# Weight conversion in place, two feed-forward pieces held over, and four first-pair copies on VectorE, in a top-k attention and hardswish kernel

## The chip, the cores and the metric

One Trainium2 chip, one of its cores. The metric is the device time of one launch in microseconds. Three runs of the kernel before took 1567.45, 1564.12 and 1565.65 us; their median, 1565.65 us, is the time before.

## What is computed

Attention over 8 batches and 8 heads (576 rows of width 64) in which each row of scores keeps only its 32 largest entries, followed by a feed-forward block with a hardswish gate over the 4608 rows that result:

```python
scores = scale * np.matmul(q, k.transpose(0, 1, 3, 2))
kth = np.partition(scores, -top_k, axis=-1)[..., -top_k:-top_k + 1]
scores = np.where(scores >= kth, scores, -1000000000.0)
scores = scores - np.max(scores, axis=-1, keepdims=True)
attn = np.exp(scores)
attn = attn / (np.sum(attn, axis=-1, keepdims=True) + 1e-09)
x = np.matmul(attn, v)             # then (B,H,S,D) -> (B*S, H*D)
h = x @ w_in                       # 512 -> 2048
g = h * np.clip(h + 3.0, 0.0, 6.0) / 6.0
out = g @ w_out                    # 2048 -> 512
```

`top_k` is 32. q, k and v are float32. The weights are float64, so each of them reaches the kernel as a pair of 32-bit words, `lo` and `hi`, and is turned into float32 on the chip.

## The kernel before

**Pairs and duos.** Two heads make a pair (`Pair`), two pairs a duo (`Duo`): one tile of 128 query rows (or the 64 rows that are left over, a "rest" duo) of four heads. There are 80 duos, ten in each batch; `m` numbers them. Even batches end with their two rest duos, odd batches begin with them.

**Slots.** The order of the work is written out by hand. The loop of L608 gives each duo eight slots, numbered 8m+i. In a slot VectorE does one round of `top` (L276): eight maxima of a row (`max`, L283) and their removal (`match_replace`, L287), for both heads of a pair; four rounds per pair find the 32 largest. The other steps of a duo hang at fixed slots after its start (the tables of L570 to L583; `usual`, `behind` for the middle of the run, `early` for the first two duos, `soon` for the last two): `shift` (GpSimd), `exp` (ScalarE, L306 to L316), `inverse` (VectorE, L320), `weights` (GpSimd, L330 and the copy of L339 that splits words into halves), `flip` (a transposing DMA on SP's queue, L345), `join` (ScalarE for the duo's first pair, GpSimd for its second, L351), `values` (TensorE, L371), `place` (ScalarE, L381, from PSUM to `xT`). `scores` of the next duo (TensorE, L256 and L262, then ScalarE's copy from PSUM, L271) are issued in slot 1 of a duo, and transposes of a later pair (L182, then copies on ScalarE, L205 to L187) in slot 5 where there is one.

**Pieces.** When both duos of a row tile are placed, `queue` (L471) adds a feed-forward block: 16 pieces. Pieces 0 to 7 compute `h` (L398, two pieces per 512 columns, then ScalarE's L406 and L408 and, two pieces later, GpSimd's gate L412 and L413); pieces 8 to 15 accumulate `acc` (L418), and the last also scales the result (ScalarE, L428) and sends it out (a DMA on SP's queue, L430). `left` counts the pieces not yet issued. At the end of each slot L639 adds 1 to `due` while `left` is over 0 (half as much in slots of a rest duo, a little more when `left` is 24 or over), and `piece` issues that many. A block is queued about every 16 slots, so `left` runs from 16 to 0 and a new block follows at once: in slot order, the block's last piece is issued just before `place` of the next block's second duo.

**Weights.** 32 chunks of 128x512 (16 of `w_in`, 16 of `w_out`) are converted one per slot in the first 33 slots (`convert`, L96; `convert_step`, L522). A chunk is loaded into a tile `st` of the pool `kq` (14 buffers, shared with all the tiles of the attention). Three slots later ScalarE writes |hi| into a tile `a` of the pool `g` (L109), GpSimd clamps it (L110), and ScalarE makes `y` from `lo` (L112); two slots after that VectorE shifts `a` (L118) and merges the sign into the destination (L119), and in the next slot GpSimd adds both (L124). `y` is a PSUM tile (pool `ps_w`, 3 buffers, shared with `h`, `acc` and `pv`) where `early` holds, else the destination itself. L518 makes `early` true for chunks 0 to 15.

**Start.** The first pair is transposed through three `ps_w` tiles (L189 to L202) and ScalarE copies the keys (L195), the first query tile (L196) and the left-over keys (L187). Scores of that pair alone follow (`us == (0,)`, L267), copied out in three parts by ScalarE.

Each engine runs its instructions in program order, and so does SP's queue of DMAs.

Of the kernel before, what the change touches and what calls it, by code (L numbers as in the profile page):

```python
# [8 lines left out]
AF = mybir.ActivationFunctionType  # L9
ALU = mybir.AluOpType  # L10
F32 = mybir.dt.float32
U32 = mybir.dt.uint32
I32 = mybir.dt.int32
# [11 lines left out]
HI_LEAST = 2.0**-15  # L25
HI_MOST = 122880.0 - 2.0**-7
# [3 lines left out]
def kernel(  # L30
# [9 lines left out]
    nc = tc.nc  # L40
    P = nc.NUM_PARTITIONS
# [3 lines left out]
    JP = J * P  # L45
    R = S - JP
    NHP = H // 2
    NFC = FF // P
# [4 lines left out]
    def pool(name, bufs, **kw):  # L53
        return ctx.enter_context(tc.tile_pool(name=name, bufs=bufs, **kw))
# [8 lines left out]
    gpool = pool("g", 8)  # L63
# [24 lines left out]
    def big():  # L88

        return ps_big.tile([P, 5 * 512], F32, tag="big", name="big")  # L90
# [3 lines left out]
    WC = 512  # L94

    def convert(dst, src, early):  # L96

        st = kqpool.tile([P, 2 * WC], U32, tag="kq", name="st")
        nc.sync.dma_start(st[:], src)
        yield
        words = st[:].rearrange("p (n two) -> p n two", two=2)
        lo, hi = words[:, :, 0], words[:, :, 1]
        a = gpool.tile([P, WC], F32, tag="g", name="a")
        y = ps_w.tile([P, WC], F32, tag="w", name="y")[:] if early else dst
        nc.scalar.activation(a[:], hi.bitcast(F32), AF.Abs)  # L109
        nc.gpsimd.tensor_scalar(a[:], a[:], HI_MOST, HI_LEAST, ALU.min, ALU.max)  # L110

        nc.scalar.activation(y, lo, AF.Copy, bias=2.0, scale=2.0**-51)  # L112
        yield

        au = a[:].bitcast(U32)
        nc.vector.tensor_scalar(au, au, 3, None, ALU.logical_shift_left)  # L118
        nc.vector.scalar_tensor_tensor(  # L119
            out=dst.bitcast(U32), in0=hi, scalar=0x80000000, in1=y.bitcast(U32),  # L120
            op0=ALU.bitwise_and, op1=ALU.bitwise_or,
        )
        yield
        nc.gpsimd.tensor_tensor(  # L124
            dst.bitcast(I32), a[:].bitcast(I32), dst.bitcast(I32), ALU.add
        )

    def weight_chunks():
# [11 lines left out]
    class Pair:  # L140
# [31 lines left out]

        def transpose(self, first=False):

            kq = kqpool.tile([P, JP + S], F32, tag="kq", name="kq")
            self.kT, self.qT = kq[:, 0:JP], kq[:, JP : JP + S]
            c0 = 2 * JP

            def turn(ps, tiles):
                for i, j in enumerate(tiles):  # L180
                    rows = self.landed[:, j, :, :].rearrange("p h d -> p (h d)")
                    nc.tensor.transpose(ps[:, i * P : (i + 1) * P], rows, ident[:])  # L182

            def copy_left(ps):
                for hh in range(2):
                    d = slice(hh * D, (hh + 1) * D)
                    nc.scalar.copy(self.kr[d, hh, :], ps[d, 0:R])  # L187

            if first:  # L189

                ps = [ps_w.tile([P, 512], F32, tag="w", name="kqp") for _ in range(3)]
                turn(ps[0], range(J))
                turn(ps[1], [J, 2 * J])
                turn(ps[2], range(J + 1, 2 * J))
                nc.scalar.copy(self.kT, ps[0][:])  # L195
                nc.scalar.copy(kq[:, JP : JP + P], ps[1][:, 0:P])  # L196
                copy_left(ps[1][:, P:])
                self.later = [
                    (kq[:, JP + P : c0], ps[2][:, 0 : JP - P]),
                    (kq[:, c0 : c0 + R], ps[1][:, P + R : 2 * P]),  # L200
                ]
                return  # L202
            ps = big()
            turn(ps, range(2 * J + 1))
            nc.scalar.copy(kq[:, 0:c0], ps[:, 0:c0])  # L205
            nc.scalar.copy(kq[:, c0 : c0 + R], ps[:, c0 + R : c0 + 2 * R])
            copy_left(ps[:, c0:])

    class Duo:
# [15 lines left out]
        def scores(self, us=(0, 1)):  # L225

            if us[0] == 0:
                self.sc = scpool.tile([P, 2, 2 * (S + R)], F32, tag="sc", name="sc")
                self.den = mpool.tile([P, 2, 2], F32, tag="den", name="den")
            sc, nu = self.sc[:, us[0] : us[-1] + 1, :], len(us)  # L230
            ps = big()
            heads = [slice(0, D), slice(D, P)]
            qs = slice(self.qt * P, min(self.qt * P + P, S))
            banks = ps[:, 0 : 4 * 512].rearrange("p (n s) -> p n s", s=512)
            left = ps[:, 4 * 512 :]
            if self.rest:


                quarters = [
                    (i, hh, d, heads[u ^ hh])  # L240
                    for i, u in enumerate(us)
                    for hh, d in enumerate(heads)
                ]
                for i, hh, d, to in quarters:
                    pr = self.pairs[us[i]]
                    nc.tensor.matmul(banks[to, i, :], pr.qT[d, qs], pr.kT[d, :])
                for i, hh, d, to in quarters:
                    pr = self.pairs[us[i]]
                    nc.tensor.matmul(banks[to, 2 + i, 0:R], pr.qT[d, qs], pr.kr[d, hh, :])
                nc.gpsimd.memset(sc[:, :, S : S + R], 0.0)  # L250
                nc.scalar.copy(sc[:, :, 0:JP], banks[:, 0:nu, :])
                nc.scalar.copy(sc[:, :, JP:S], banks[:, 2 : 2 + nu, 0:R])
                return
            for i, u in enumerate(us):
                pr = self.pairs[u]
                nc.tensor.matmul(  # L256
                    left[:, i * P : (i + 1) * P], pr.qT[:, qs], pr.kr[:].rearrange("p h r -> p (h r)")
                )
            for i, u in enumerate(us):
                pr = self.pairs[u]  # L260
                for hh, d in enumerate(heads):
                    nc.tensor.matmul(banks[:, 2 * i + hh, :], pr.qT[d, qs], pr.kT[d, :])  # L262
            copies = [
                (sc.rearrange("p u (h s) -> p (u h) s", h=2)[:, :, 0:JP], banks[:, 0 : 2 * nu, :]),
                (sc[:, :, JP : JP + P], left[:, 0 : nu * P].rearrange("p (u r) -> p u r", r=P)),
            ]
            if us == (0,):  # L267
                (to, src), rest = copies
                copies = [rest, (to[:, 0, :], src[:, 0, :]), (to[:, 1, :], src[:, 1, :])]
            for copy in copies:  # L270
                nc.scalar.copy(*copy)  # L271

        def row(self, u, t):
            return self.sc[:, u, t * S : (t + 1) * S]
# [171 lines left out]
    ND = len(duos)  # L446
# [4 lines left out]
    left = 0  # L451
# [60 lines left out]
    chunks = list(weight_chunks())  # L512
    landing, converting, adding = [], [], []

    def land(count=1):

        for _ in range(min(count, len(chunks))):
            c = convert(*chunks.pop(0), early=len(chunks) >= NFC)  # L518
            next(c)
            landing.append(c)  # L520

# [26 lines left out]
    ps = big()  # L548
    for _ in range(2):
        nc.tensor.matmul(ps[:, 0:DM], w_out[:, 0, 0:P], w_out[:, 0, :])  # L550
    first[0].load(nc.scalar)
    first[1].load()
    land()
    first[2].load()
    land()
    first[0].transpose(first=True)
    duos[0].scores((0,))
    for copy in first[0].later:
# [17 lines left out]
    early = dict(  # L576
        shift0=3, exp0=3, inverse0=4, weights0=4, flip0=5, join0=8,
        shift1=7, exp1=7, inverse1=8, weights1=8, flip1=9, join1=12, values=12, place=13,
    )
# [27 lines left out]
    due = 0.0  # L607
    for m in range(ND + 3):  # L608
        u = duos[m] if m < ND else None
        for i in range(8):  # L610
            if u:
                u.top(i // 4, i % 4)
            if m < 4:
                parts(8 * m + i, False)
            convert_step()
            if m == 0 and i in (1, 2):
                first[i + 1].transpose()
            if i == (4 if m == 0 else 1) and m + 1 < ND:
                duos[m + 1].scores()
            if m < 4:  # L620
                parts(8 * m + i, True)
            else:
                parts(8 * m + i)
            if m == 0 and i in (1, 4):
                for p in duos[i // 4].pairs:
                    p.load_values()
            if i == 0:
                p = pair_at(m, 4)
                if p:
                    p.load()  # L630
            if i == 3 and u and u.pairs[0].b and 1 <= m % per_batch <= 2:
                for p in duos[m - 1].pairs:
                    p.load_values()
            if i == 5:
                p = pair_at(m, 5)
                if p:
                    p.transpose()

            due += ((left > 0) + (left >= 24) / 8 + (left >= 48) / 8) / (2 if u and u.rest else 1)  # L639
            piece(int(due))  # L640
            due -= int(due)
    while todo:
# [35 lines left out]
```

## Time and profile before

| what | us |
|---|---|
| median of three runs (lowest, highest) | 1565.65 (1564.12, 1567.45) |
| the profiled execution, whole time | 1564.01 |
| its span, first to last instruction | 1562.2 |
| VectorE busy in it | 1467.0 |
| TensorE busy in it | 1443.5 |
| GpSimd busy in it | 1137.8 |
| ScalarE busy in it | 1096.0 |
| `h` and `acc` on TensorE (L398, L418) | 1066.7 |
| conversion on VectorE (L118, L119) | 54.6 |

The profiled execution is 1.64 us under the median. Two engines are busy for over nine tenths of the span. The durations of a group can add up to more than its engine's busy time, because an instruction's start overlaps the end of the one before. In the lines of a timeline the columns are the start in us, the duration in us, engine, line, operation, what is written from what is read, shapes and count; in brackets stands the idle time of that engine just before and what ended it. "SPq" is SP's queue of DMAs.

### The profile page before, as it was taken

Reading aid. Unit: us, or ns where it says so; the run is one execution under the profiler, and the core shown is the slowest. Engines: PE = TensorE matmul, PEld = TensorE weight load, DVE = VectorE, ACT = ScalarE, POOL = GpSimd, SP = SyncE. Lnnn points to the kernel's source line nnn. Section 1 sums busy time; section 2 is a strip of 40 time slices with the busy share of each in tenths; the row PEclk is TensorE's granted clock in tenths of the full one; section 3 lists DMA queues with packets and bytes.
Section 4 is the critical chain, followed back from the end, with each engine's and each line's share of the span. In section 5 each row is a group of like instructions: output and inputs, shape, how many; then the busy total and the mean of one; then the engine's idle time right before and its main releaser. Section 6 shows DMA issues by size and latency. Waiting matters only on the chain.

```text
span 1562.2 us, 28737 instructions
## 1 busy us (share of the span) xinstructions
PE 1443.5 (92%) x10276; PEld 1030.4 (66%) x10276; DVE 1467.0 (94%) x3106; ACT 1096.0 (70%) x1868; POOL 1137.8 (73%) x1264
## 2 busy tenths in 40 slices
PE   5266798899999999999999999999999999999899
PEld 3152665677777777667767777677777777667665
DVE  6999999999999998999999999999999999999910
ACT  6784776677777777777777776777777777777631
POOL 4778688677777788677777778777777778677761
PEclk7667899999999999999999999999999999999999
DMA  8643445344344445344344454455343455433420
GB/s 225 191 167 68 92 84 109 78 92 83 69 84 98 99 84 104 75 100 100 70 85 84 100 99 83 90 99 98 69 83 83 99 99 92 96 68 68 77 44 14
DMA packets 450319, 144.49 MB, mean 92 GB/s; under 512 B 433280, under 2 KB 441472, under 8 KB 450176
## 3 DMA queue, kind: packets, MB, share of 16 engines
q1 hardware_dynamic: 448976, 142.36, 44.2%
q8 instruction: 81, 1.33, 0.3%
q14 instruction: 62, 0.51, 0.1%
q10 hardware_dynamic: 1200, 0.30, 0.1%
HBM read 45.09 MB, written 9.44 MB: 35 GB/s over the span
## 4 chain that ended last, share of the span: by engine, by line
PE 50%; DVE 32%; POOL 6%; ACT 4%; issue 4%; DMA 1%; SPq 1%; POOLq 0%; ACTq 0%
PE h L398 20%; PE acc L418 19%; DVE m L283 16%; DVE wk L287 13%; PE pv L371 6%; PE big L262 5%; POOL e L339 2%; POOL sc L330 1%; POOL eT L351 1%; DMA t<-e 1%; PE big L182 1%; PE big L256 1%; DVE w_out L119 1%; DVE a L118 1%; POOL g L413 1%
## 5 line engine op out<-in xcount | busy, mean ns | idle before, releaser
L283 DVE MAX8 m<-wk 128x8 f32<-128x576 f32 x864 | 613.2, 746 | 2.2
L418 PE MATMUL acc<-w_out,g 128*128 128x512 f32 x1152 | 521.4, 603 | 10.5 <-POOL g L413 10.5
L398 PE MATMUL h<-xT,w_in 128*128 128x128 f32 x4096 | 483.6, 278 | 14.0 <-ACT xT L381 11.7
L398 PEld LDWEIGHTS h<-xT,w_in 128*128 128x128 f32 x4096 | 470.3, 193 | 39.7 <-issue 19.3
L287 DVE MATCH_REPLACE8 wk<-m,wk 128x576 f32<-128x576 f32 x576 | 423.7, 742 | 0.0
L418 PEld LDWEIGHTS acc<-w_out,g 128*128 128x128 f32 x1152 | 214.1, 192 | 255.4 <-issue 234.0
L330 POOL TENSOR_SCALAR sc<-sc,den 128x576 f32<-128x576 f32 x288 | 212.8, 748 | 205.7 <-DVE den L320 174.0
L339 POOL COPY e<-sc 128x2304 uint16<-128x2304 uint16 (+1 forms) x192 | 320.1, 1677 | 10.1
L306 ACT ACTIVATE sc<-sc,m 128x576 f32<-128x576 f32 x288 | 210.5, 778 | 71.2 <-DVE m L283 71.1
L351 ACT COPY eT<-t 128x2304 uint16<-128x2304 uint16 (+1 forms) x82 | 216.0, 2635 | 56.3 <-DMA t<-e 55.9
L311 ACT ACTIVATE sc<-sc,shift 128x576 f32<-128x576 f32 x288 | 220.4, 770 | 34.1 <-POOL shift L299 31.9
L371 PE MATMUL pv<-eT,vm 128*64 128x128 f32 (+1 forms) x2560 | 163.8, 272 | 62.0 <-ACT eT L351 24.3
L287 DVE MATCH_REPLACE8 wk<-m,sc 128x576 f32<-128x576 f32 x288 | 211.9, 742 | 0.0
L283 DVE MAX8 m<-sc 128x8 f32<-128x576 f32 x288 | 203.3, 743 | 8.8 <-ACT sc L271 8.8
L371 PEld LDWEIGHTS pv<-eT,vm 128*64 128x64 f32 x2560 | 134.8, 141 | 114.2 <-ACT eT L351 27.4
L351 POOL COPY eT<-t 128x2304 uint16<-128x2304 uint16 (+1 forms) x78 | 203.5, 2608 | 7.0 <-DMA t<-e 6.9
L406 ACT ACTIVATE g<-h,three 128x512 f32<-128x512 f32 x144 | 98.8, 686 | 136.5 <-PE h L398 136.1
L413 POOL TENSOR_TENSOR g<-g,hs 128x512 f32<-128x512 f32 x144 | 184.3, 1280 | 12.0
L271 ACT COPY sc<-big 128x256 f32<-128x256 f32 (+3 forms) x131 | 136.6, 1095 | 31.4 <-PE big L262 31.2
L412 POOL TENSOR_SCALAR g<-g 128x512 f32<-128x512 f32 x144 | 88.9, 618 | 73.2 <-ACT g L406 63.8
L262 PE MATMUL big<-kq 64*128 64x512 f32 x512 | 132.6, 637 | 0.0
L408 ACT COPY hs<-h 128x512 f32<-128x512 f32 x144 | 83.7, 581 | 0.0
(57 smaller groups left out, 999.2 us busy)
## 6 DMA issues: line engine op xcount, KB each, us to landing
landed<-in_k_dram SPq DMA_DIRECT2D x64, 128.0 KB, 2.9
st<-in_moe_w_in_dram SPq DMA_DIRECT2D x16, 512.0 KB, 5.4
vm<-in_v_dram SPq DMA_DIRECT2D x64, 128.0 KB, 2.4
st<-in_moe_w_out_dram SPq DMA_DIRECT2D x16, 512.0 KB, 6.3
out_dram<-o SPq DMA_DIRECT2D x32, 256.0 KB, 2.5
landed<-in_q_dram SPq DMA_DIRECT2D x62, 128.0 KB, 2.8
t<-e SPq DMA_TRANSPOSE x160, 4.6
landed<-in_k_dram SPq DMA_DIRECT2D x32, 32.0 KB, 2.5
```

What stands on the lines that cost most here:

```text
L262: nc.tensor.matmul(banks[:, 2 * i + hh, :], pr.qT[d, qs], pr.kT[d, :])
L283: nc.vector.max(self.m[u][:, t, 8 * r : 8 * r + 8], self.cur[t])
L287: nc.vector.match_replace(wk, self.m[u][:, t, 8 * r : 8 * r + 8], self.cur[t], LOWEST)
L306: nc.scalar.activation(row, row, AF.Prelu, bias=m[:, t, TOP_K - 1 : TOP_K], scale=-1.0, alpha=FLAT)
L311: nc.scalar.activation(row, row, AF.Exp, bias=self.less[u][:, t : t + 1], scale=-scale / FLAT, accum_out=self.den[:, u, t : t + 1],)
L330: nc.gpsimd.tensor_scalar(row, row, self.den[:, u, t : t + 1], 1.0, ALU.mult, ALU.mult)
L339: nc.gpsimd.tensor_copy(halves[:, :, to : to + c1 - c0], words)
L351: copy(eT[:, 0 : self.nb, :] .rearrange("p c q -> p (c q)") .bitcast(U16) .rearrange("p (x h) -> p h x", h=2), self.t16[u][:, 0 : 2 * self ...
L371: nc.tensor.matmul(pv[hh * D : (hh + 1) * D, u * w : (u + 1) * w], pr.vm[:, hh, c, :] if c < J else pr.vr[:, hh, :], rhs, start=(c == 0), ...
L398: nc.tensor.matmul(h[:, (f - f0) * P : (f - f0 + 1) * P], w_in[:, i, f * P : (f + 1) * P], xT[:, i, :], start=(i == 0), stop=(i == NHP - 1),)
L413: nc.gpsimd.tensor_tensor(g[:], g[:], hs[:], ALU.mult)
L418: nc.tensor.matmul(acc[:], gs[f // nf][:, f % nf * P : (f % nf + 1) * P], w_out[:, f, :], start=(f == 0), stop=(f == NFC - 1),)
```

## The change

Six edits:

1. `convert`: the tile `a` is gone. ScalarE makes `y` from `lo` first, and then writes |hi| over `lo`, in every second word of `st`. GpSimd's clamp, VectorE's shift and GpSimd's sum work there, at a step of 8 bytes. `st` is in use until the sum.
2. `land`: `y` is a PSUM tile for chunks 0 to 23 instead of 0 to 15.
3. `transpose(first=True)`: the copies of the first query tile and of the left-over keys are VectorE's instead of ScalarE's.
4. `scores((0,))`: of the three copies VectorE takes the one of the left-over columns (128x128).
5. The main loop: a slot adds to `due` only while `left` is over 2, but over 0 from the last duo's slots on.
6. `copy_left` takes the engine's copy as an argument (for 3).

```diff
         words = st[:].rearrange("p (n two) -> p n two", two=2)
         lo, hi = words[:, :, 0], words[:, :, 1]
-        a = gpool.tile([P, WC], F32, tag="g", name="a")
         y = ps_w.tile([P, WC], F32, tag="w", name="y")[:] if early else dst
-        nc.scalar.activation(a[:], hi.bitcast(F32), AF.Abs)
-        nc.gpsimd.tensor_scalar(a[:], a[:], HI_MOST, HI_LEAST, ALU.min, ALU.max)
 
         nc.scalar.activation(y, lo, AF.Copy, bias=2.0, scale=2.0**-51)
+
+        a = lo.bitcast(F32)
+        nc.scalar.activation(a, hi.bitcast(F32), AF.Abs)
+        nc.gpsimd.tensor_scalar(a, a, HI_MOST, HI_LEAST, ALU.min, ALU.max)
         yield
...
-        au = a[:].bitcast(U32)
-        nc.vector.tensor_scalar(au, au, 3, None, ALU.logical_shift_left)
+        nc.vector.tensor_scalar(lo, lo, 3, None, ALU.logical_shift_left)
         nc.vector.scalar_tensor_tensor(
             out=dst.bitcast(U32), in0=hi, scalar=0x80000000, in1=y.bitcast(U32),
             op0=ALU.bitwise_and, op1=ALU.bitwise_or,
         )
         yield
         nc.gpsimd.tensor_tensor(
-            dst.bitcast(I32), a[:].bitcast(I32), dst.bitcast(I32), ALU.add
+            dst.bitcast(I32), lo.bitcast(I32), dst.bitcast(I32), ALU.add
         )
...
-            def copy_left(ps):
+            def copy_left(ps, copy=nc.scalar.copy):
                 for hh in range(2):
                     d = slice(hh * D, (hh + 1) * D)
-                    nc.scalar.copy(self.kr[d, hh, :], ps[d, 0:R])
+                    copy(self.kr[d, hh, :], ps[d, 0:R])
...
-                nc.scalar.copy(kq[:, JP : JP + P], ps[1][:, 0:P])
-                copy_left(ps[1][:, P:])
+                nc.vector.tensor_copy(kq[:, JP : JP + P], ps[1][:, 0:P])
+                copy_left(ps[1][:, P:], nc.vector.tensor_copy)
...
             for copy in copies:
-                nc.scalar.copy(*copy)
+                if us == (0,) and copy is rest:
+                    nc.vector.tensor_copy(*copy)
+                else:
+                    nc.scalar.copy(*copy)
...
-            c = convert(*chunks.pop(0), early=len(chunks) >= NFC)
+            c = convert(*chunks.pop(0), early=len(chunks) >= NFC // 2)
...
-            due += ((left > 0) + (left >= 24) / 8 + (left >= 48) / 8) / (2 if u and u.rest else 1)
+            due += ((left > (2 if m < ND - 1 else 0)) + (left >= 24) / 8 + (left >= 48) / 8) / (2 if u and u.rest else 1)
```

## The prediction

> **What bounds the kernel now.** I read the engines' totals first.
>
> ```profile
> PE 1443.5 (92%) x10276; PEld 1030.4 (66%) x10276; DVE 1467.0 (94%) x3106; ACT 1096.0 (70%) x1868; POOL 1137.8 (73%) x1264
> ```
>
> TensorE (PE) and VectorE (DVE) are both nearly full, so the question is which one paces the other. The list of VectorE's waits answers it (total, times, longest):
>
> ```profile
> DVE den L320 <- ACT den L316: 14.1, 4, 5.9
> DVE m L283 <- ACT sc L271: 8.8, 1, 8.8
> DVE a L118 <- POOL a L110: 1.1, 2, 0.8
> ```
>
> Between its first maximum at 10.24 us and its last at 1491 VectorE stands still for only 9.3 us: 1.1 before two conversions and 2.34, 3.66 and 2.15 before three reciprocals (the fourth, 5.92, comes when the top-k is over). It never waits for scores again, so TensorE's own stalls cost VectorE nothing, except where they hold ScalarE. VectorE's end is the sum of its own work and those waits. After it come 71 us of tail, looked at last. The timeline of the start:
>
> ```profile
> 12.47 0.67 ACT L109 ACTIVATE a<-st 128x512 f32<-128x512 f32 x1 [1.27 <-DMA st<-in_moe_w_in_dram]
> ...
> 13.22 0.61 POOL L110 TENSOR_SCALAR a<-a 128x512 f32<-128x512 f32 x1 [10.18 <-ACT a L109]
> ...
> 13.87 0.43 DVE L118 TENSOR_SCALAR a<-a 128x512 uint32<-128x512 uint32 x1 [0.76 <-POOL a L110]
> ...
> 32.22 0.17 DVE L320 RECIPROCAL den<-den 128x2 f32<-128x2 f32 x1 [2.34 <-ACT den L316]
> ```
>
> VectorE's second step hangs on a weight chunk's landing through ScalarE and GpSimd (POOL), and it waits again at 32.22 for ScalarE, whose own chain goes back to another landing (its L109 at 22.70 follows 2.48 us of waiting for `st`).
>
> **Start: 0.** VectorE's new copies take three instructions (0.27 + 2 x 0.21 us by ScalarE's rows L196 and L187) and one of 0.27 off ScalarE; VectorE has no such row. Bounds 0.2 and 0.7 us each; I take ScalarE's, for the work is the same. They lie in its 8.83 us of idleness, and the first maximum comes up to 0.8 us earlier. But `a` now follows `y`: it starts at 13.04 instead of 12.47, so the clamp and L118 move by +0.57, to 14.44. What the copies win is waited off there. The +0.57 is in turn swallowed by the 2.34 us at 32.22, whose releaser doesn't move. If that cover is gone: +0.57.
>
> **Conversions: -0.7.** The timeline shows what a conversion costs beside GpSimd:
>
> ```profile
> 54.31 1.44 POOL L124 TENSOR_TENSOR w_in<-a,w_in 128x512 int32<-128x512 int32 x1
> 54.55 0.67 DVE L119 SCALAR_TENSOR_TENSOR w_in<-st,y 128x512 uint32<-128x512 uint32 x1
> ...
> 56.42 1.27 POOL L124 TENSOR_TENSOR w_in<-a,w_in 128x512 int32<-128x512 int32 x1
> 56.49 1.48 DVE L118 TENSOR_SCALAR a<-a 128x512 uint32<-128x512 uint32 x1
> ...
> 85.75 1.75 DVE L119 SCALAR_TENSOR_TENSOR w_out<-st,w_out 128x512 uint32<-128x512 uint32 x1
> ```
>
> The shift L118 takes 0.41 us where GpSimd is idle, and 1.48 where an addition began 0.07 before it: it waits that one out. L119 takes 0.67 in spite of GpSimd when `y` is in PSUM, up to 1.75 when both inputs are in SBUF. (a) Chunks 16 to 23 get `y` in PSUM. Their L119 rows are 0.68, 0.68, 1.75, 1.09, 0.68, 1.09, 0.68, 0.68 = 7.33; at 0.676, the mean of the 16 with PSUM, 5.41: -1.9. The price is in the pool of three PSUM tiles. In slot 21 `y` of chunk 23 waits for L119 of chunk 21 (over at 99.8), some 2 us on ScalarE; behind it are L109, L112 and a ReLU that idles 3.36 us before 103.02. Hidden; without that cover it would delay the exponentials of slot 24 by 2. (b) L118 at a step of 8 bytes has no row. One end is L118 itself, the other L119, which reads `hi` at that step in 0.67 and isn't held: the 28 after 32 us took 23.6 and would take 19.0, -4.6. If the step costs 0.27 and the waiting stays, 28 x 0.27 = +7.6. I take no change, as operation and memories are the same. (c) GpSimd at that step: 0, or a third more as its L351 (1.21 ns an element) stands to L339 (0.91); L124 grown by 0.42 in some eight waits is +3.4. I take 0. (d) GpSimd's clamp comes later. In slot 8, where it had waited 1.80 us for ScalarE, the weighting after it moves from 50.71 to 51.1, and so does the copy that L118 of slot 10 waits out: +0.41, in three such groups, +1.2. (e) `st` is held one slot longer. The loads of chunks 22 to 31 leave at 88.4 to 100.2, and the next transposing DMA behind them has its data at 121.55: hidden. Sum -1.9 + 1.2 = -0.7, bounds -6.5 and +9.
>
> The Trainium skill, "Vector Engine (DVE) Microarchitecture Reference", section "Performance modes", gives the two-port mode to one-source operations with input and output in SBUF and asks for no unit step; "SBUF — State Buffer", section "SBUF: two separate sides", says that such an instruction and GpSimd exclude each other. By that rule (no row here shows that step) the in-place form keeps the 0.41 and the waiting, (b) is 0, and the -4.6 is ruled out.
>
> **Pieces kept back, mid-run: -3.7.** TensorE's stalls at a new block (11.7 us on `xT`, 6.7 on `xr`, 2.3 on `o`, 27 times) get two pieces as cover. That is no gain by itself, since VectorE paces. One place is different, a batch boundary where half-rate slots put a block's last piece into slot 227:
>
> ```profile
> 585.29 0.60 ACT L428 ACTIVATE o<-acc 128x512 f32<-128x512 f32 x1 [3.25 <-PE acc L418]
> ...
> 586.38 8.21 SPq L345 DMA_TRANSPOSE t<-e  x3
> 592.23 2.79 ACT L351 COPY eT<-t 128x2304 uint16<-128x2304 uint16 x1 [3.15 <-DMA t<-e]
> ...
> 598.12 0.17 DVE L320 RECIPROCAL den<-den 128x1 f32<-128x1 f32 x1 [3.66 <-ACT den L316]
> ```
>
> SP's queue sits on the output of that piece until 585.91; the flip behind it (slot 228) had its data at 581.40. It lands 5.83 after issue, ScalarE waits for it with an exponential behind, and VectorE stands for 3.66. Two pieces later the last piece falls into slot 231 and its output behind that flip: the flip leaves at 581.5, lands at 587.3, the join ends at 590.1, `o` at 590.7, the exponential's sum at 592.6, before VectorE's 594.46. The whole 3.66 goes; the bound is 0. The next flip (slot 232, data at 588.24) now stands behind the output, until 591.0, 1.7 late; its join on GpSimd runs to 599.6 instead of 597.9, and what is late next, a reciprocal at 605.6, has 1.9 us left.
>
> **Tail: +3.25.**
>
> ```profile
> 1486.50 1.09 PE L371 MATMUL pv<-eT,vm 128*64 128x128 f32 x16 [4.07 <-POOL eT L351]
> ...
> 1487.74 5.36 PE L418 MATMUL acc<-w_out,g 128*128 128x512 f32 x8
> ...
> 1492.05 2.77 POOL L351 COPY eT<-t 128x2304 uint16<-128x2304 uint16 x1
> ...
> 1494.87 1.09 PE L371 MATMUL pv<-eT,vm 128*64 128x128 f32 x16 [0.53 <-POOL eT L351]
> ```
>
> TensorE waits for GpSimd's joins, the last at 1494.8, and from there works without a gap to 1558.4. GpSimd is busy end to end from VectorE's reciprocal at 1465.31, so that point moves with VectorE. The threshold falls to 0 with slot 632, but the rate stays one piece a slot: at `values` of slot 640 two pieces fewer are done. Old order after it: pieces 14, 15; new: 12 to 15. Two pieces are 3.6 us (8 matmuls, 3.60). The gates come two slots later on GpSimd, a weighting earlier, and the 0.16 us and smaller gaps before it close: the join ends some 0.35 earlier. +3.25. Bounds: 0, if TensorE gets to them before, and +5.0: after the 4.07 us of idleness the granted clock is 0.62 and 0.81 in the two stretches of 3 us that follow, and eight matmuls take 5.36 instead of 3.60, 1.76 more. I take none, since after idling for the join before, the clock has those 6 us to recover.
>
> The Trainium skill, "TensorE: Matmul & The Clock Gate", section on the HAM clock gate, has the clock halved after an idle window of some 3.4 us; it speaks against keeping work back, and if it strikes at 1494 the tail is +5.
>
> **Sum.** 0 - 0.7 - 3.7 + 3.25 = -1.15. The profiled execution took 1564.0 (span 1562.2), so 1562.9; it lies 1.6 under the median of 1565.65, to which the same step gives **1564.5**.
>
> **Rivals.** A: the strided shift no longer waits for GpSimd. For it: L119's 0.67 beside a busy GpSimd. Against: that row has a PSUM input. -4.6 more: 1559.9. B: the stalls come off the end, because TensorE paces. For it: the chain of waits gives PE 50%. Against: no wait of VectorE for scores. Of the 20.7 us the part on `xT`, some 12: 1565.65 - 12 = 1553.5. C, slower: the kept pieces only move the harm. The output now in front of the flip of slot 232 holds that one, so the 3.66 stays, and the pieces come after the last join on a slow clock: -0.7 + 3.25 + 1.76 = +4.3, 1570. It decides if the output waits beyond 593 and TensorE idles over 4 us before 1494. For it: the output waited up to 27.6 us elsewhere; against: TensorE gets to that piece with less work ahead of it.
>
> **How the numbers follow.** Forecast 0.40, A 0.20, B 0.12, C 0.28. A measurement here can tell 0.2%, 3.1 us, from nothing: faster is under 1562.5, slower over 1568.8. The forecast's own range is 1561 to 1568.5: faster 0.10, same 0.28, slower 0.02. A gives 0.17 and 0.03, B 0.12 faster, C 0.26 slower and 0.02 same. Faster 0.39, same 0.33, slower 0.28. The range, 1556 to 1573, takes in A, C and most of (c), and leaves out most of B and the far end of (b).
>
> **What would show it.** Right: L118 still near 0.41 alone and over 1 beside GpSimd; L119 of chunks 16 to 23 at 0.67; no reciprocal waiting near 595; four pieces instead of two after the last second `values` wait. Wrong: L118 constant near 0.65 (A); VectorE's end unmoved while the tail shrinks (B); a reciprocal still waiting after the boundary, or a clock under 1 after 1494 (C).

## The result, and the profile after

The changed kernel took 1565.27 us (median of six runs, 1562.62 to 1566.83) against 1565.39 for the kernel before in the same comparison: ratio 0.9995, 95% interval 0.9981 to 1.0009. No difference can be told. The forecast had been 1564.5 with a range of 1556 to 1573. The profiled execution took 1564.38 us (span 1562.6), 0.4 more than the one before (1564.01, span 1562.2), not 1.15 less, so its terms have to be looked at one by one. From the page of after, the engines' totals and the chain of work that ended last:

```profile
PE 1437.9 (92%) x10276; PEld 1025.2 (66%) x10276; DVE 1465.6 (94%) x3110; ACT 1102.7 (71%) x1864; POOL 1137.3 (73%) x1264
...
DVE 78%; PE 10%; issue 4%; POOL 4%; ACT 2%; DMA 1%; SPq 1%; POOLq 0%; DVEq 0%; ACTq 0%
```

The chain was half TensorE and a third VectorE before; now 78% of it is VectorE. TensorE's waits for `xT` at a new block have nearly gone, and the end has not moved with them. Before and after, in total, times, longest:

```profile
PE h L398 <- ACT xT L381: 11.7, 22, 1.0
PE h L404 <- ACT xT L387: 2.2, 1, 2.2
```

VectorE's waits of after, in the same columns:

```profile
DVE den L326 <- ACT den L322: 9.6, 2, 7.9
...
DVE st L118 <- POOL st L113: 2.5, 3, 0.9
```

Four waits for ScalarE's sum became two. Those of 3.66 at 598.12 and of 2.15 at 1477.32 are gone; the last, when the top-k is over, grew from 5.92 to 7.94. The timeline of after, at the places of the start and of the conversions that the prediction had read:

```profile
13.90 0.43 DVE L118 TENSOR_SCALAR st<-st 128x512 uint32<-128x512 uint32 x1 [0.88 <-POOL st L113]
...
24.37 1.31 POOL L124 TENSOR_TENSOR w_in<-st,w_in 128x512 int32<-128x512 int32 x1
24.46 1.51 DVE L118 TENSOR_SCALAR st<-st 128x512 uint32<-128x512 uint32 x1
...
31.96 0.17 DVE L326 RECIPROCAL den<-den 128x2 f32<-128x2 f32 x1 [1.70 <-ACT den L322]
```

The shift at a step of 8 bytes takes 0.43 alone, and 1.51 where an addition of GpSimd started 0.09 before it: as fast as before, and it waits as before. The conversion's groups, shapes kept apart (total us, mean ns):

```profile
L118 DVE TENSOR_SCALAR st<-st 128x512 uint32<-128x512 uint32 x32 | 28.7, 898 | 2.5 <-POOL st L113 2.5
L113 POOL TENSOR_SCALAR st<-st 128x512 f32<-128x512 f32 x32 | 23.3, 728 | 43.6 <-ACT st L112 39.1 <-DMA st<-in_moe_w_in_dram 3.9
...
L119 DVE SCALAR_TENSOR_TENSOR w_out<-st,w_out 128x512 uint32<-128x512 uint32 x8 | 7.2, 905 | 0.0
L119 DVE SCALAR_TENSOR_TENSOR w_out<-st,y 128x512 uint32<-128x512 uint32 x8 | 5.4, 674 | 0.0
```

With 10.8 for `w_in`, L118 and L119 take 52.1 us where they took 54.6. L118 rose by 2.3 (26.4 before); L119 on `w_out` fell by 4.8 (17.4 before). The batch boundary:

```profile
574.17 8.27 SPq L351 DMA_TRANSPOSE t<-e  x2
...
587.10 0.15 DVE L326 RECIPROCAL den<-den 128x1 f32<-128x1 f32 x1
587.20 0.60 ACT L434 ACTIVATE o<-acc 128x512 f32<-128x512 f32 x1
587.83 0.36 SPq L436 DMA_DIRECT2D out_dram<-o  x1
588.29 16.69 SPq L351 DMA_TRANSPOSE t<-e  x4
592.71 0.15 DVE L326 RECIPROCAL den<-den 128x1 f32<-128x1 f32 x1
```

The output (`o` at 587.20) now stands behind the flip that it used to hold, and no reciprocal waits. VectorE's reciprocals are 1.66 earlier than before ahead of the boundary (587.10 against 588.76) and 5.4 behind it (598.32 against 603.68). The tail:

```profile
1479.11 1.09 PE L377 MATMUL pv<-eT,vm 128*64 128x128 f32 x16 [3.17 <-POOL eT L357]
...
1482.47 1.41 DVE L289 MAX8 m<-wk 128x8 f32<-128x576 f32 x2
...
1489.50 1.98 PE L377 MATMUL pv<-eT,vm 128*64 128x128 f32 x16 [4.21 <-POOL eT L357]
...
1491.84 8.37 PE L424 MATMUL acc<-w_out,g 128*128 128x512 f32 x16
```

VectorE's last maximum is 7.4 us earlier, the last wait for a join 5.37 earlier (1489.50 against 1494.87). Behind it the program needs 73.1 us instead of 67.3: two more pieces, and slow ones, 8.37 for sixteen matmuls. Busy times by stretch, with the granted clock in the column behind POOL's:

```profile
1487.00:1490.00 3.00, 0.50 (x6) 0.50 (x8) 0.00 (x0) 0.08 (x1) 2.79 (x3) 0.59 0.67 125
1490.00:1493.00 3.00, 3.00 (x20) 2.15 (x19) 0.17 (x1) 2.79 (x7) 0.93 (x2) 0.50 0.00 0
1493.00:1496.00 3.00, 3.00 (x7) 1.28 (x6) 0.00 (x0) 2.00 (x1) 2.65 (x2) 0.77 0.00 0
```

TensorE works through the second and third stretch at a granted clock of 0.50 and 0.77. So: 5.37 won in front of the last join, 5.8 lost behind it.

### The profile page after: what moved, and what is told of

The parts are those of the page before. It is cut to its first block, busy times and chain, and to the rows that moved or that the text cites. A ratio compares the mean times of both kernels' runs of the same rounds, so it can differ in the third digit from the quotient of the medians.

```text
span 1562.6 us, 28772 instructions
## 1 busy us (share of the span) xinstructions
PE 1437.9 (92%) x10276; PEld 1025.2 (66%) x10276; DVE 1465.6 (94%) x3110; ACT 1102.7 (71%) x1864; POOL 1137.3 (73%) x1264
## 3 DMA queue, kind: packets, MB, share of 16 engines
q8 instruction: 81, 1.33, 0.4%
## 4 chain that ended last, share of the span: by engine, by line
DVE 78%; PE 10%; issue 4%; POOL 4%; ACT 2%; DMA 1%; SPq 1%; POOLq 0%; DVEq 0%; ACTq 0%
DVE m L289 41%; DVE wk L293 35%; PE acc L424 4%; PE h L404 4%; POOL e L345 1%; PE pv L377 1%; POOL sc L336 1%; DVE den L326 1%; DVE st L118 1%; ACT sc L317 1%; ACT eT L357 1%; POOL w_out L124 1%; PE big L265 0%; DVE w_in L119 0%; SPq L153 0%
## 5 line engine op out<-in xcount | busy, mean ns | idle before, releaser
L404 PE MATMUL h<-xT,w_in 128*128 128x128 f32 x4096 | 475.8, 277 | 4.3 <-ACT xT L387 2.2
L277 ACT COPY sc<-big 128x2048 f32<-128x2048 f32 (+3 forms) x130 | 136.2, 1099 | 3.5 <-DVE sc L275 2.3
```

Of the source, the lines that this page charges most:

```text
L404: nc.tensor.matmul(h[:, (f - f0) * P : (f - f0 + 1) * P], w_in[:, i, f * P : (f + 1) * P], xT[:, i, :], start=(i == 0), stop=(i == NHP - 1),)
```

## The experiments

Twelve kernels, each timed against the kernel before on the same chip: first for the boundary and the tail, then for the conversions.

**keep_only**: the kernel before with edit 5 alone.

```diff
-            due += ((left > 0) + (left >= 24) / 8 + (left >= 48) / 8) / (2 if u and u.rest else 1)
+            due += ((left > (2 if m < ND - 1 else 0)) + (left >= 24) / 8 + (left >= 48) / 8) / (2 if u and u.rest else 1)
```

> The kernel before with edit 5 alone (two pieces kept back). Theory: the reciprocal that waited 3.66 us at 598.12 no longer waits and stands near 594.5, VectorE's last maximum ends some 3.7 to 5.7 us before that of the kernel before (1491.2), the last wait for a join ends near 1490.5 to 1491, and the work behind it is 5.8 us longer (two pieces at 1.8 and some 2 us of lower clock), so the span is 1562 to 1564.5: no change to +2. Rival (TensorE paces, covered stalls come off the end): 10 us or more faster, under 1553. Rival (output only moves in front of the next flip): the reciprocal still waits and the span is 1567 to 1568.

Measured: 1565.34 us, ratio 1.0005 (0.9996 to 1.0014). The wait at the boundary and the one of 2.15 are gone; VectorE's last maximum ends at 1485.2, 6.1 earlier. The tail, in the timeline of keep_only:

```profile
1480.41 1.97 PE L371 MATMUL pv<-eT,vm 128*64 128x128 f32 x16 [3.15 <-POOL eT L351]
...
1490.82 1.09 PE L371 MATMUL pv<-eT,vm 128*64 128x128 f32 x16 [1.38 <-POOL eT L351]
...
1492.06 7.13 PE L418 MATMUL acc<-w_out,g 128*128 128x512 f32 x16
```

Here the slow stretch came after the first of the two joins, where TensorE had time to spare, and the sixteen matmuls behind the last took 7.13. The work behind the last join is 1561.6 - 1490.82 = 70.8 us, 3.5 more than before and not the 5.8 expected: what two pieces cost, without a slow clock behind the last join.

**no_keep**: the changed kernel without edit 5 (the line of keep_only turned back).

> The changed kernel without edit 5. Theory: the conversions and the start alone bring VectorE 1.5 to 2 us ahead; the wait of 3.66 us in the rest duos stays; the tail behind the last join keeps its 67.3 us; span 1560 to 1561, 1.5 to 2 us under before. If conversions and start were worth nothing, the reciprocals stand where they stood before and the span is 1562.

Measured: 1565.93 us, ratio 1.0013 (1.0003 to 1.0024). The wait at the boundary is there, and longer (5.12 at 603.67), so edit 5 is what takes it away. But the reciprocal in front of it came at 592.91, 4.15 later than before, not earlier: L119 on the last eight chunks took 13.4 us, not the 7.2 of after. The profiled execution was one of the longest of ten, 1569.71; three lay at 1569.6 to 1569.7, seven at 1564.3 to 1566.6.

**out_queue**: the kernel before with the output's DMA on ScalarE's queue.

```diff
-                nc.sync.dma_start(dst, o[p0:p1, :])
+                nc.scalar.dma_start(dst, o[p0:p1, :])
```

> The kernel before with the output DMA issued from ScalarE's queue instead of SP's. Theory (the stall of 3.66 us comes from the flip that stands behind the output in SP's queue): the flip leaves at 581.5 instead of 586.4, the reciprocal near 595 doesn't wait, VectorE ends 3.7 to 5.7 us earlier, and as the pieces stay where they were, the tail isn't longer: span 1557 to 1559. Rival (the stall comes from ScalarE standing 3.25 us before the last scaling of the block, behind TensorE): the flip leaves early but the reciprocal still waits 2 us or more, span 1560 to 1562.

Measured: 1575.09 us, ratio 1.0068 (1.0051 to 1.0085). The wait of 3.66 went, but four others stand near it (1.19, 1.82, 2.29 and 1.83 between 562.86 and 602.83), and VectorE waits for ScalarE's sum 14 times instead of 4, 25.4 us in all. The expectation was missed: ScalarE runs in order too, and more hangs on it, as I read the 14 waits. It doesn't separate the cause at the boundary; that rests on keep_only and no_keep.

**catch_up**: the changed kernel, with the threshold of 2 only up to duo 71, and an eighth of a piece more per slot in duos 72 and 73, so that the two pieces are made up before the end.

```diff
-            due += ((left > (2 if m < ND - 1 else 0)) + (left >= 24) / 8 + (left >= 48) / 8) / (2 if u and u.rest else 1)
+            due += ((left > (2 if m < ND - 8 else 0)) + (left >= 24) / 8 + (left >= 48) / 8) / (2 if u and u.rest else 1)
+            if ND - 8 <= m < ND - 6:
+                due += 1 / 8
             piece(int(due))
```

> The changed kernel with the kept-back pieces issued in the last batch: the threshold is 2 only up to duo 71, and 1/8 is added to due in the 16 slots of duos 72 and 73, so that from slot 594 on the pieces stand in the slots of the kernel before. Theory: VectorE as in the changed kernel up to there (reciprocal at 592.7, no wait), work behind the last join back to 67 to 68 us, span 1556.5 to 1558.5, faster than both by some 5 us. If the longer tail of the changed kernel has another cause than the two pieces, it stays at 73 us and the span at 1562.

Measured: 1559.29 us, ratio 0.9967 (0.9957 to 0.9977). Behind the last join (1490.30) there are 67.3 us again, and no reciprocal waits at the boundary. The longer tail of the changed kernel, its slow clock included, hangs on the two pieces, and it can be avoided.

**catch_up4**: catch_up with the same eighth in duos 78 and 79 too.

```diff
-            if ND - 8 <= m < ND - 6:
+            if ND - 8 <= m < ND - 6 or ND - 2 <= m < ND:
```

> The version catch_up, with an eighth of a piece more due also in the slots of duos 78 and 79, so that four pieces in all are made up before the last second `values` wait: the order behind that wait is that of before less two further pieces. Theory (the longer tail is nothing but pieces left over, on a TensorE that otherwise waits for GpSimd's joins): work behind the last join falls from 67.3 to about 63.7 us, the time by 3.0 to 3.6 against catch_up (1559.3), to 1555.5 to 1556.5. Rival (the pieces before the join delay the transposes or scores that VectorE's last maxima need, or ScalarE's exponential): VectorE's last maximum moves from 1485.3 to 1487 or later, and the time stays at 1559. Second rival (TensorE idles longer in the middle and is given a slower clock at the end): `acc` x16 behind the last join takes over 8 us instead of 7.2.

Measured: 1554.27 us, ratio 0.9933 (0.9919 to 0.9948). The timeline of its tail:

```profile
1480.94 1.09 PE L377 MATMUL pv<-eT,vm 128*64 128x128 f32 x16 [1.70 <-POOL eT L357]
...
1488.10 1.09 PE L377 MATMUL pv<-eT,vm 128*64 128x128 f32 x16 [0.97 <-POOL eT L357]
...
1489.34 14.56 PE L404 MATMUL h<-xT,w_in 128*128 128x128 f32 x128
```

63.9 us are left behind the last join (1552.0 - 1488.10), as expected. The time fell by more than the pieces: the join itself is 2.2 earlier than in catch_up, where TensorE had waited 4.05 before the join ahead of it and ran 16 matmuls in 1.97; here it waited 1.70 and they took 1.09. Of the 2.2 VectorE was 1.05 ahead already at the boundary (a reciprocal at 586.81, in catch_up at 587.86), which the added eighths at the end can't have brought.

**in_place_only**: the kernel before with edit 1 alone (the first three hunks of the change).

> Kernel before with edit 1 alone (|hi| written over `lo`, no tile `a`). Theory: the shift at a step of 8 bytes costs what it did at 4 (0.41 to 0.43 us alone, over 1 beside GpSimd), GpSimd's sum 1.30 to 1.37; the later clamp costs VectorE 1.2 us; L119 of the `w_out` chunks stays near 17.4 us in 16; the reciprocal before the stall comes at 589 to 591 (before 588.76) and the stall after it stays at 3.5 to 5: 1565.5 to 1566.5. Rival (the loss of no_keep, whose VectorE stood 4 us late by 560 us, sits here, because sum and shift of the last chunks now meet): L119 of `w_out` 19 us or more, the reciprocal at 592 or later, time 1567 to 1568. Rival A (the strided shift isn't held by GpSimd): L118 19 us in 32, time 1560 to 1561.

Measured: 1569.02 us, ratio 1.0026 (1.0014 to 1.0038): this part is a loss, larger than theory and rival had it. The reciprocal comes at 591.93, 3.17 later; L118 takes 28.8 us (+2.4), L119 on `w_out` 18.3 (+0.9). The timeline of before at slot 10:

```profile
52.24 2.10 POOL L339 COPY e<-sc 128x2304 uint16<-128x2304 uint16 x1
53.44 1.19 DVE L118 TENSOR_SCALAR a<-a 128x512 uint32<-128x512 uint32 x1
```

and of in_place_only:

```profile
53.56 2.10 POOL L337 COPY e<-sc 128x2304 uint16<-128x2304 uint16 x1
53.98 1.96 DVE L116 TENSOR_SCALAR st<-st 128x512 uint32<-128x512 uint32 x1
```

The shift waits out GpSimd's copy in both. The copy is later because the clamp ahead of it now follows two instructions of ScalarE, not one: 1.19 became 1.96, and so at three places four slots apart (0.49 to 1.26, 1.19 to 1.96, 1.19 to 1.98).

**psum_only**: the kernel before with edit 2 alone.

```diff
-            c = convert(*chunks.pop(0), early=len(chunks) >= NFC)
+            c = convert(*chunks.pop(0), early=len(chunks) >= NFC // 2)
```

> Kernel before with edit 2 alone (`y` in PSUM for chunks 16 to 23 too). Theory: the eight L119 of these chunks take 0.68 each, 5.4 us in all instead of 7.3; VectorE is 1.9 us earlier from 100 us on (reciprocal at 586.9 instead of 588.76), the stall after it stays: 1562.5 to 1563.5. Rival (what is won there is lost in the last eight chunks, whose L119 with both inputs in SBUF then meet GpSimd's copies): these eight take 11 us or more (before 10.1), and the reciprocal comes at 588 to 592: 1564 to 1567.

Measured: 1562.44 us, ratio 0.9984 (0.9967 to 1.0001). In the profiled execution (1565.17) chunks 16 to 23 took 5.4 us and the last eight 13.3, the rival's case; the reciprocal came at 588.37. Five of ten runs lie at 1559.5 to 1560.9 and five at 1564.0 to 1568.5.

**start_only**: the kernel before with edits 3, 4 and 6 (the hunks of `copy_left`, of the first pair and of `copies`).

> Kernel before with edits 3, 4 and 6 alone (first-pair copies on VectorE). Theory: VectorE's first maximum comes 0.3 to 0.8 us earlier, L118 of the first chunk at its landing as before (13.3 to 14.0), the wait at the reciprocal near 32 takes the rest: 0, 1564 to 1565, reciprocal at 588.5 to 589. Rival (ScalarE's lighter start carries through to its exponential at 31 us): the wait at 32 falls from 2.34 to 1.7 and all that follows is 0.6 earlier: 1563.8. Second rival (a shift of the slots' start by some tenths of a us redraws which VectorE instruction meets which of GpSimd's in the 32 conversions): L118 and L119 together change by 2 us or more in either direction, with nothing in the conversion edited.

Measured: 1564.51 us, ratio 0.9995 (0.9985 to 1.0004). Conversions as before (26.3 and 28.2 us), the wait near 32 still 2.34, and the wait at the boundary 4.33 with one of 1.56 in front of it. Two expectations were missed in the profiled execution: the first maximum came at 11.91, 1.67 later than before and not earlier, and the reciprocal at 590.66. The first was not the copies' doing: TensorE's nine first transposes took 2.15 us instead of 1.42, as they also did in psum_only, whose start is that of before (first maximum at 11.79). At the reciprocal near 32 only 0.28 of it was left. In the time nothing is won or lost that can be measured.

The sum of the three parts at the reciprocal before the boundary (before 588.76; in_place_only +3.17, psum_only -0.39, start_only +0.34 if its wait of 1.56 there is left out) doesn't give the changed kernel's -1.66. What differs is the last eight chunks. The timeline of no_keep, where the first of them is shifted:

```profile
109.67 0.66 POOL L113 TENSOR_SCALAR st<-st 128x512 f32<-128x512 f32 x1 [1.40 <-ACT st L112]
109.95 0.67 DVE L118 TENSOR_SCALAR st<-st 128x512 uint32<-128x512 uint32 x1
110.30 1.48 POOL L124 TENSOR_TENSOR w_out<-st,w_out 128x512 int32<-128x512 int32 x1
110.54 1.79 DVE L119 SCALAR_TENSOR_TENSOR w_out<-st,w_out 128x512 uint32<-128x512 uint32 x1
```

and of after:

```profile
109.59 0.41 DVE L118 TENSOR_SCALAR st<-st 128x512 uint32<-128x512 uint32 x1
109.66 1.49 POOL L113 TENSOR_SCALAR st<-st 128x512 f32<-128x512 f32 x1 [1.74 <-ACT st L112]
109.93 0.68 DVE L119 SCALAR_TENSOR_TENSOR w_out<-st,w_out 128x512 uint32<-128x512 uint32 x1
```

GpSimd comes at the same time in both, since ScalarE in front of it waits for the same matmuls (`h`, over at 107.1 in both). VectorE is 0.36 apart, and that from the start, where a load decides it: ScalarE had waited for the landing of the second chunk until 16.67 us in no_keep, until 16.34 in after. By 0.07 us VectorE is first in after: GpSimd waits, 1.49 instead of 0.66, and VectorE's next steps stay in front of it. In no_keep GpSimd is first, and its addition, already at 110.30, is waited out by L119. The Trainium skill, "SBUF — State Buffer", section "SBUF: two separate sides", says that whichever of the two starts first has the ports for its whole instruction; these rows agree (the shift takes 0.41 where it comes first and 0.67 where it comes second). Two kernels tested whether that order, and not edit 5, decides.

**late_dve**: the changed kernel with one more VectorE instruction ahead of the shift of chunk 24 (`n` is the chunk's number).

```diff
+        if n == 24:
+            nc.vector.max(spot[:], w_out[:, 0, 0:288])
         nc.vector.tensor_scalar(lo, lo, 3, None, ALU.logical_shift_left)
```

> The changed kernel with one more VectorE instruction, a maximum of 128x288, about 0.4 us, ahead of the shift L118 of chunk 24 (109.59 us in after). Theory (a race of 0.1 us decides what the last eight L119 cost): in after that shift starts 0.07 before GpSimd's clamp L113 of chunk 25, which then waits, and the eight L119 with both inputs in SBUF take 7.2; 0.4 later GpSimd is first, as in no_keep (109.67 against 109.95), and the eight take 12 to 13.5. VectorE is then 0.4 + 5 to 6 later at its reciprocals (592.5 to 593.5 instead of 587.1) and at its end; time 1568 to 1571, ratio 1.002 to 1.0035. Rival (edit 5, which moves gates of the first block on GpSimd, is what made those eight cheap): they stay at 7 to 8.5, reciprocal at 587.5, time 1565 to 1566.

Measured: 1567.59 us, ratio 1.0007 (0.9996 to 1.0019); the profiled execution took 1568.17. Its timeline:

```profile
109.92 0.45 DVE L120 MAX8 spot<-w_out 128x8 f32<-128x288 f32 x1
110.06 0.68 POOL L114 TENSOR_SCALAR st<-st 128x512 f32<-128x512 f32 x1 [1.82 <-ACT st L113]
110.29 0.73 DVE L121 TENSOR_SCALAR st<-st 128x512 uint32<-128x512 uint32 x1
...
110.94 1.79 DVE L122 SCALAR_TENSOR_TENSOR w_out<-st,w_out 128x512 uint32<-128x512 uint32 x1
```

The last eight L119 took 13.5 us, and the reciprocal before the boundary came at 593.18, 6.1 later than in after, for 0.45 us of added work, with edit 5 in place. VectorE came to this place at 109.92, 0.33 later than in after, and GpSimd at 110.06, 0.40 later: without the added instruction the shift would have been first by 0.14, so it is what turned the order. The profiled time rose by 3.8 only, since the slow clock now fell on the first of the last joins (70.8 us are left behind the last, 73.1 in after); the median is under the range expected.

**late_act**: no_keep with `y` of chunk 25 made twice, so that GpSimd's clamp comes later.

```diff
+        if n == 25:
+            nc.scalar.activation(y, lo, AF.Copy, bias=2.0, scale=2.0**-51)
         a = lo.bitcast(F32)
```

> no_keep (after without edit 5) with one more ScalarE instruction, `y` of chunk 25 made twice (0.67 us), so that GpSimd's clamp of chunk 25 starts near 110.3 instead of 109.67 and VectorE's shift of chunk 24 (109.95) goes first. Theory (the same race): the last eight L119 fall from 13.4 to 7 to 9 us, the reciprocals before the boundary come at 586.5 to 589 instead of 592.9, the stall behind them stays (3.5 to 5), time 1560.5 to 1563 though an instruction was added. Rival (edit 5 decides): the eight stay at 12 to 13.4, reciprocal at 592.5 to 593.5, time 1565.5 to 1566.5.

Measured: 1565.8 us, ratio 1.0003 (0.9994 to 1.0013). Its timeline:

```profile
110.23 0.42 DVE L120 TENSOR_SCALAR st<-st 128x512 uint32<-128x512 uint32 x1
110.56 0.68 DVE L121 SCALAR_TENSOR_TENSOR w_out<-st,w_out 128x512 uint32<-128x512 uint32 x1
111.82 0.69 POOL L115 TENSOR_SCALAR st<-st 128x512 f32<-128x512 f32 x1 [3.28 <-ACT st L114]
```

The last eight took 8.3 us without edit 5, and the reciprocal came at 588.97, 3.9 earlier than in no_keep's profile. So the cheap order doesn't need edit 5. That the added instruction brought it about isn't shown. The clamp came 2.15 later than in no_keep, and the instruction is 0.7 of that; the rest stood in front of it, where ScalarE waits for `h`, in no_keep and in late_act:

```profile
107.12 0.69 ACT L412 ACTIVATE g<-h,three 128x512 f32<-128x512 f32 x1 [2.81 <-PE h L404]
```

```profile
108.52 0.69 ACT L414 ACTIVATE g<-h,three 128x512 f32<-128x512 f32 x1 [3.95 <-PE h L406]
```

From 105 to 108 us TensorE's granted clock was 1.00 in no_keep and 0.60 in late_act, so `h` was done later. Without the added instruction the clamp would have come near 111.1, behind the shift at 110.23 all the same. The time missed the expectation: 1560.5 to 1563 was reckoned from no_keep's profiled execution, which had the dear order (1569.71); most runs of no_keep were some 4 us shorter already, and the median didn't move. It may be that the order differs from run to run of one kernel. That the two groups in the runs of psum_only and no_keep are the two orders fits their distance, but only profiled executions have a trace, so it isn't shown.

**keep_catch4**: the kernel before with edit 5 and the catching up of catch_up4, without edits 1 to 4 and 6.

> Kernel before with edit 5 and the catching up of catch_up4, without edits 1 to 4 and 6: what the conversion and start edits are worth in the fastest version. Theory (they are worth what the draws of the conversions give, here L118 + L119 26.3 + 28.2 = 54.5 us in keep_only against 52.2 in catch_up4, and the start's 0.3): VectorE's end at 1485 (catch_up4 1485.7), four pieces made up, time 1554 to 1556, within 0.1% of catch_up4's 1554.3. Rival (the edits carry part of the gain): 1557 or more.

Measured: 1555.63 us, ratio 0.9938 (0.9923 to 0.9954), beside 0.9933 for catch_up4. All that these versions win comes from the pieces; the other edits of the change together add nothing that can be told from no change.

**psum_keep4**: keep_catch4 with edit 2.

> keep_catch4 (before, edit 5, four pieces made up at the end) with edit 2, without the in-place conversion. Theory (edit 1 costs VectorE 3.2 us, as in in_place_only, through shifts that wait out one more GpSimd instruction; edit 2 takes off 1.9 in chunks 16 to 23 and 1.8 in shifts; the last eight L119 are a draw of 7 to 8 or 13 us): L118 near 24.6 us, `st,y` on w_out 5.4 in 8, reciprocal near 588.4 with the slow draw and 583 with the fast one (keep_catch4 588.43); time 1550 to 1552 in the fast draw, 1555 to 1556 in the slow one, so a median of 1550 to 1556 with the runs in two groups some 4 to 5 us apart. Rival (VectorE is no longer what sets the end once four pieces are made up): the time stays at 1554.3 to 1556 in all runs, with VectorE's last maximum earlier and TensorE's waits at the last joins gone.

Measured: 1551.22 us (three runs at 1551.0 to 1551.4 and one at 1556.69), ratio 0.9924 (0.9905 to 0.9944): the shortest of all, 0.8% under the kernel before. L118 took 23.8 us (26.3 in keep_catch4) and the last eight L119 8.2; VectorE's last maximum is at 1481.13, where keep_catch4 had 1485.90, and the span fell by the same 4.7 (1554.0 to 1549.3). So VectorE still sets the end, against the rival. The run at 1556.69 stands where keep_catch4 does; how much of the gain is edit 2 and how much the cheap order of the last eight, four runs don't tell.

## Why the prediction was right, and where its terms were off

The forecast of 1564.5 held, and so did the outcome that goes with it, no difference to be told, though the chances had put faster (0.39) ahead of the same (0.33). Its sum of -1.15 was +0.4 in the profiled execution: a tail dearer by 2.5 than forecast and a conversion part better by 1.0 partly cancelled. That the time fits so well is in part luck, the more so as the better conversion part rests on the order of two instructions (below).

**Start: 0.** Right in the sum. VectorE's copies took 0.29, 2 x 0.22 and 0.29 in its idle time, but the first maximum came only 0.10 earlier (10.14). L118 came at 13.90 and not at 14.44, since ScalarE could begin with the chunk at 11.81 instead of 12.47; in no_keep, with the same edits at the start, it came at 14.68. The wait near 32 swallowed such differences, as the prediction had it. start_only shows no change that can be measured.

**Conversions: -0.7 taken, -1.66 measured.** The mechanisms of (a), (b) and (c) held: L119 of chunks 16 to 23 at 0.674 (-1.9), the strided shift at 0.41 to 0.43 and still waiting, GpSimd's clamp 0.728 where it was 0.731 and its sums 1.33 and 1.37 where they were 1.30 and 1.32. Of the price that (a) named, ScalarE's wait for a PSUM tile, 0.9 us came. One count in (b) is off: there are 27 shifts after 32 us, 23.2 us, and 28 only from 28.87 us on, which moves the refused -4.6 by 0.2. (d) was too small: in the three groups the shift took 1.25, 1.97 and 1.98 instead of 0.49, 1.19 and 1.19, so 0.76 to 0.79 each and not 0.41, 2.3 in all; L118's total rose by the same. And a term was missing: the last eight L119 took 7.2 instead of 10.1. That is not a gain of any edit but an order of two instructions, decided by 0.07 us: late_dve turns it over with edit 5 in place, and late_act has the cheap order without edit 5. L118 and L119 together gave -2.5; waits for the clamp took back 1.4 (2.5 against 1.1), the wait at 32 gave 0.64 (1.70 against 2.34): -1.7.

**Boundary: -3.7 taken, -3.7 measured.** Right, place and size. In seven kernels with edit 5 no reciprocal waits there; in the six without it that keep the output on SP's queue the wait is 3.66 to 5.13. That the flip behind the output in SP's queue is the way it works is read from the rows: ScalarE's join waited 3.15 for the flip before and 1.66 after. Edit 5 also took away ScalarE's 3.25 in front of `o`, and no run parts the two. The second stall, 2.15 at 1477.32, also went, which the prediction had not said; it brought nothing, as the last reciprocal waited 2.02 longer. That is why VectorE's end moved by 7.4 (1.66 + 3.66 + 2.15) and the last join by 5.37 only (1.66 + 3.7).

**Tail: +3.25 taken, +5.8 measured.** This is the term that was most off. The two pieces cost the 3.6 us (3.5 in keep_only). The 0.35 that the join was to come earlier beside VectorE did not show, and the 1.76 for a slow clock, named as the bound and refused, came true as 2.2 (5.8 - 3.6; by the tails of after and keep_only 73.1 - 70.8 = 2.3). The argument failed at "the clock has those 6 us to recover". It presumed that the idleness before the earlier join would slow the clock there, and that TensorE would reach the last join late. In after TensorE waited 3.17 us before the earlier join at a clock of 1.00 and did the eight matmuls behind it in 3.70 instead of 5.36, 1.66 less. The earlier join had moved up by 7.39 and the last by 5.37 only, 2.02 more between them. So TensorE stood 4.21 us before the last one and not 0.53, and nothing hides a slow matmul behind it. keep_only, with the same pieces, had the slow clock at the earlier join, as the argument had it, and the tail of 70.8.

**Rivals.** A is refuted: L118 rose to 28.7. B is refuted: `xT` stalls of 9.5 us went and the end did not move with them. Of C the half on the queue is refuted; the half on the clock was right in the profiled execution of after, and with it the changed kernel gives back what it wins.

## What to carry to other kernels

Work kept back as cover is owed at the end: a threshold that is lifted in the last stage needs a rate above one there, and here making up the two pieces turned no difference into 0.3% (catch_up), and making up two more into 0.7% (catch_up4). Where VectorE and GpSimd meet within tenths of a microsecond, a difference of some microseconds between two profiles can be an order of arrival and not the edit, so read several runs, and push the order on purpose before explaining it. Taking away a stall pays only as far as the same engine doesn't wait again later: count the waits behind it.

## What the runs showed of the hardware that was not expected

0.45 us added to VectorE at one place went with a loss of 6.1 us by the next boundary (late_dve against after), through the order of VectorE and GpSimd; 0.33 of it was there before the added instruction.

The granted clock did not follow the length of a wait alone: after 3.17 us without work it stayed at 1.00 (after, 1479.11), after 3.15 it was 0.50 from 1480 to 1486 (keep_only), and after 2.13 it was 0.50 from 1478 to 1481 (psum_keep4) and from 1483 to 1485 (keep_catch4). The stretches, the clock again behind POOL's column, of after and of psum_keep4:

```profile
1478.00:1481.00 3.00, 1.89 (x22) 1.48 (x23) 3.00 (x8) 1.64 (x5) 2.83 (x3) 1.00 0.00 0
```

```profile
1478.00:1481.00 3.00, 3.00 (x21) 2.16 (x18) 3.00 (x8) 0.37 (x1) 2.39 (x3) 0.50 0.01 3
```

The Trainium skill, "TensorE: Matmul & The Clock Gate", section "Part 1: The HAM clock gate", gives an idle window of some 3.4 us that runs freely. From that it would follow that the place of the gap in the window counts, and these rows agree with it. They don't agree with the length: gaps of 2.13 us sufficed twice, so TensorE needn't be idle for 3.4 us without a break.
